# Another order of the seven outer products in the down projection of a retention + SwiGLU kernel, with split inner sums and a last unit that is finished block by block

## The chip, the cores and the metric

The kernel runs on one core of a Trainium2 chip. A core has five engines that each work through their own list of instructions in order: TensorE (PE in the profile; its weight loads are PEld), VectorE (DVE), ScalarE (ACT), GpSimd (POOL) and SyncE (SP, which here only issues transfers). They wait for one another through semaphores. Matmuls write to PSUM, eight banks of 128 x 512 f32; everything else lies in SBUF. The metric is the device time of one execution in microseconds (us).

## The reference, cut to what matters

```python
# q, k, v: (8 batches, 8 heads, 576 positions, 64), f32
scores = q @ k.T / sqrt(64);  ret = scores * gamma_h ** (i - j)  for j <= i, else 0
x = (ret @ v) as (8*576 = 4608 tokens, 8*64 = 512 channels)
xn = x / sqrt(mean(x*x) + 1e-6) * rms_g
h = silu(xn @ w_gate) * (xn @ w_val)      # 4608 x 1536
out = h @ w_out                           # 4608 x 512
```

Nearly all of the arithmetic is in the two projections of the last two lines.

## The kernel before, in words

**Units.** The 4608 tokens are worked through in nine units of 512 (u = 0 to 8). A unit has an up part (gate and value projection, six groups `up(u, n)`) and a down part, `across(u)`. Attention for later units is done in slots between the up groups. All program text from `start` on is under a manual schedule: the order in which the Python emits instructions is the order on each engine. Units 0 and 1 take their up part plainly (`up_plain`, L664), while the weights are still being rounded and combined; this front is emitted by the string `PLAN`, whose entries stand for pieces of work: `w` and `a` steps of weight rounding on VectorE and ScalarE, `U` a plain up group (u, k, n), `S` an attention slot, `d` differences of h, `i` inner sums of unit 0, `W36` "all 36 weight halves joined", `A0`/`A1` the next half outer product of unit 0 or 1, `R2 Y2 X2 M2` the normalisation of unit 2 and its mixtures. For units 2 to 8 a loop (from L1113) takes over.

**Seven products in place of eight.** A 2x2 block product is formed with seven block products (Winograd's form of Strassen's scheme). Down is done so on two levels. Outer: h (128 x 12 x 512) is read as b11, b12, b21, b22 (channel halves by token halves), and the operands of the seven outer products are A11 = b11, A12 = b21, S4 = b22, S1 = b12 − b11 (in the spare tile t1, `differences`, L688), S3 = b22 − b12 (in b12's place, same line), S2 = S3 + b11 (overwrites b11 after the first product, L803), and A22 = b21 − S2 (overwrites t1 after the second, L805). In `operands_of` this is a table from name to tile. Inner: every outer operand is itself split in four, of which three quarters are used raw and four are sums i1, i3, i2, i4, made by `inner_sums(u, n)`, four operations over 128 x 384 (three channel blocks of 128 tokens). Sums lie in `inner[:, 0 or 1]` in turn, those of the third product in `sums_x`. From unit 2 on they run on GpSimd, those of n = 1 on VectorE (`eng`, L720).

**An outer product** is 21 matmuls of 128 x 128 x 128 over three channel blocks (L749): first the three raw quarters (18 records in the trace), then the four sums (24 records), accumulating into seven 128 x 128 places in a pair of PSUM banks, `o` with four places and `p` with three. So `zo<-ring,t` is the product whose raw operand is t1, and `zo<-ring,vi` its part on inner sums. Banks are called x, z, w, y, and the order of n = 0 to 6 on them is x z w y x z w: a repeated letter accumulates onto the earlier product. ScalarE copies x to the f32 tile `vec` (`keep`, L763); VectorE adds the other banks (`add`, L770). Four blocks of `vec` then hold the inner products of the four output blocks, which `combine` turns into out rows: seven 128 x 512 additions on GpSimd, for the last unit seven 128 x 128 additions per block on VectorE (L848). `store` writes them, on SP's queue, in the last unit also on ScalarE's.

**What sets the order.** Weight blocks stream through a ring in SBUF: `pieces` lists them in order of use, `refill` (L573) issues a transfer on SP when the place is free. When an inner sum, a bank or a tile of h is overwritten, the writer waits for the last reader. `across(u)` yields between half products, so that front and loop can put other work between: of the next unit root and normalisation (L521), mixtures (`sums_of_x`, L533).

```python
nm = "xzwyxzw"[n]
product(n, nm, w, False)                     # raw quarters
product(n, nm, w, True)                      # inner sums
if u > 1 and n in (0, 1, 3, 4):
    inner_sums(u, {0: 3, 1: 4, 3: 5, 4: 6}[n])   # sums of a later product
```

Of the kernel before, what the change touches and what calls it, by code (L numbers as in the profile page):

```python
# [41 lines left out]
def kernel(  # L42
# [499 lines left out]
    ORDER = (A11, S1, S3, S2, A12, S4, A22)  # L542
    pieces = [("out", 0, n) for n in range(7)] + [("out", 1, n) for n in range(3)]
# [13 lines left out]
    def refill(most=len(pieces)):  # L557

        nonlocal n_sent
        while n_sent < min(most, len(pieces)):  # L560
# [7 lines left out]
            if kind == "up":  # L568
                src = w_up_d[n]
            else:  # L570
                o = o.rearrange("p (c x) -> p c x", c=NK)
                src = w_out_d[ORDER[n]].rearrange("c p x -> p c x")
# [3 lines left out]
    def piece(kind, u, n):  # L576
        i = pieces.index((kind, 0 if kind == "out" and u == 1 and n > 2 else u, n))
# [111 lines left out]

    def s2_of(u):  # L690
        return flat_t[1].rearrange("p (f t) -> p f t", t=HU)

    def operands_of(u):
# [4 lines left out]
        other = s2_of(1), flat_t[0].rearrange("p (f t) -> p f t", t=HU)  # L698
        s2, a22 = other if u == 1 else (b11, t1)
        return {A11: b11, S1: t1, S3: b12, S2: s2, A12: b21, S4: b22, A22: a22}  # L700

    def inner_of(u, n):
        if u > 1 and n == 2:
            t = sums_x.rearrange("p i c t -> p (i c t)")
            return list(t.rearrange("p (i c t) -> i p c t", i=4, c=NK))
        at = (0, 1, None, 0, 1, 0, 1)[n] if u > 1 else (7 * u + (n + 4 * u) % 7) % 2
        return [inner[:, at, i] for i in range(4)]

    def inner_sums(u, n):

        x = operands_of(u)[ORDER[n]]
# [3 lines left out]
        eng = nc.vector if (n == 1 if u > 1 else 7 * u + (n + 4 * u) % 7 in (4, 7, 10, 12)) else nc.gpsimd  # L715
        for o, a, b, op in (
            (i1, x12, x11, ALU.subtract), (i3, x22, x12, ALU.subtract),
            (i2, i3, x11, ALU.add), (i4, x21, i2, ALU.subtract),
        ):
            eng.tensor_tensor(out=o, in0=a, in1=b, op=op)  # L720

    def across(u):
# [8 lines left out]
        first = set()  # L731

# [4 lines left out]
        def product(n, nm, w, late):  # L737
# [3 lines left out]
            x = operands[ORDER[n]]  # L741
# [19 lines left out]
        def keep(b, nm):  # L761
            for o, ps in parts(vec[:, b], nm):
                nc.scalar.copy(out=o, in_=ps)  # L763
# [7 lines left out]

        last = u == NU - 1
        if u > 1:
            for n in range(3):
                inner_sums(u, n)
        yield
        for i, n in enumerate((3, 4, 5, 6, 0, 1, 2) if u == 1 else range(7)):
            nm = "xzwyxzw"[n]
            w = piece("out", u, n)
            product(n, nm, w, False)  # L780
# [4 lines left out]
            if u == 1:  # L785
                if i in (2, 3):
                    for at, v in ((0, "x"), (3, "y")) if i == 2 else ((2, "z"), (1, "w")):
                        keep(at, v)
                        first.difference_update([(v, 0), (v, 1)])
                elif n == 0:  # L790
                    add(0, 0, "x")
                    add(3, 3, "x")
                    plus(1, 3)
                    plus(2, 3)
                elif n == 1:
                    add(2, 2, "z")
                    add(3, 3, "z")
                elif n == 2:
                    add(1, 1, "w")
                    add(3, 3, "w")  # L800
            elif n == 0:
                keep(3, "x")
                nc.vector.tensor_tensor(out=b11, in0=b12, in1=b11, op=ALU.add)  # L803
            elif n == 1:
                nc.vector.tensor_tensor(out=t1, in0=b21, in1=b11, op=ALU.subtract)  # L805
            elif n == 3:
                add(1, 3, "y")
                add(3, 1, "z")
                add(3, 3, "w")
                if last:  # L810
                    combine(3)
            elif n == 4:
                keep(0, "x")
                if last:
                    combine(0)
            elif n == 5:
                add(2, 1, "z")
                if last:
                    combine(2)
            elif n == 6:  # L820
                add(1, 1, "w")
                if last:
                    combine(1)
            if u == 0 and n == 3:
                o = operands_of(1)
                nc.vector.tensor_tensor(out=o[S2], in0=o[A11], in1=o[S3], op=ALU.add)
            elif u == 0 and n == 6:
                nc.vector.tensor_tensor(out=o[A22], in0=o[A12], in1=o[S2], op=ALU.subtract)
            if u > 1:
                if n in (0, 1, 3, 4):  # L830
                    inner_sums(u, {0: 3, 1: 4, 3: 5, 4: 6}[n])
            elif 7 * u + i + 2 < 14:
                v, i = divmod(7 * u + i + 2, 7)
                inner_sums(v, (i + 3) % 7 if v else i)
# [16 lines left out]

    def store(u, b=None):
# [3 lines left out]
        for i, (n, r, c) in enumerate(((A12, 0, 0), (S4, 0, 1), (S3, 1, 1), (A22, 1, 0))):  # L856
# [3 lines left out]
            else:  # L860
                queue = nc.scalar if i % 2 else nc.sync
                queue.dma_start(out=rows[c][r][:, b // 2, b % 2], in_=vec[:, b, n])
# [112 lines left out]
    def finish_slice(k):  # L975
# [3 lines left out]
            (w_out_d[o][k], slices[:, o].rearrange("p n d -> p (n d)")) for o in ORDER  # L979
        ]))  # L980

    def store_blocks(n):
# [17 lines left out]
        a1 U132 a1 w1 U133 a1 w1 w1 w1 w1 w1 U040 U041 F10 w1 a1 w1 w1 U042 a1 a1 a1 a1 a1 a1 a1  # L1000
        a1 w1 w1 w1 U043 a1 a1 a1 a1 w1 w1 U050 a1 a1 a1 w1 a1 a1 a1 w1 U051 w1 a1 a1 a1 w1 a1
        w1 U052 a1 w1 U053 w1 a1 w1 w1 w1 W36 U140 a1 a1 a1 S8 P10 U141 S9 F11 a1 a1 U142 z0
        U143 a1 a1 a1 r1 a1 a1 a1 a1 a1 d1 d0 a1 U150 a1 a1 a1 a1 S10 U151 a1 r2 P11 U152 a1 a1
        i0 d2 U153 a1 A0 d5 d4 a1 S11 i1 A0 d3 A0 C11 r99 A0 A0 A0 a1 Q8 A0 G8 Q9 A0 Q10 F12 G9
# [158 lines left out]
```

## Time and profile before

| what | value |
|---|---|
| time, median of 3 runs | 1126.14 us (1125.84 to 1126.41) |
| profiled execution | 1123.96 us, span 1122.0, granted TensorE clock 0.996 |
| start of across in unit 0, 1, 4, 8 | 237.5, 273.9, 513.9, 1082.7 |
| an outer product that waits for nothing | 4.69 us |
| last matmul ends, last VectorE operation ends | 1115.5, 1119.3 |
| last store issued, landed | 1119.3, 1120.9 |

Times in the rows are microseconds from the start of the span. A timeline row gives start, length, engine, line and operation, `out<-in`, the shape, the number of instructions drawn together, and in brackets the idle time before it and what ended that. A row of stretches gives, from a start to an end, the length and then for each engine its busy time with the number of instructions, the TensorE clock (1.00 is full), DMA share and GB/s. `tile` rows give the number, the least, median and greatest duration in ns, and the first and last start. Units 2 to 7 are the middle units; unit 4 stands for them in the rows shown.

### The profile page before, as it was taken

What the parts mean: (1) busy time and instruction counts of PE and PEld (TensorE: products, weight loads), DVE (VectorE), ACT (ScalarE), POOL (GpSimd) and SP (SyncE); (2) the same over time, 40 slices, a digit from 0 to 9 for tenths busy, and PEclk for the clock granted to TensorE, in tenths of its full rate; (3) what the DMA queues carried; (4) which work ended last, traced back from release to release, by engine and by line L of the source; (5) the groups of instructions that cost most, each with busy time, mean ns of one, the idle gap of its engine ahead of it and who ended that gap; (6) DMA issues with size and microseconds to landing.
All of it is one profiled execution on the core that took longest, in us unless ns stands there. A gap on an engine that the chain in (4) does not pass through costs nothing. (4 is left out here: it accounts for less than half of the span.)

```text
span 1122.0 us, 24228 instructions
## 1 busy us (share of the span) xinstructions
PE 1095.8 (98%) x10102; PEld 914.7 (82%) x10102; DVE 797.6 (71%) x1383; ACT 272.9 (24%) x551; POOL 397.5 (35%) x328
## 2 busy tenths in 40 slices
PE   8799999999999999999999999999999999999997
PEld 7654444579988899889988898889888998898897
DVE  4768767997777795769577777778576935594465
ACT  5656465211112301121122202130122011201110
POOL 0024526566630065005800391028301740183035
PEclk8999999999999999999999999999999999999999
DMA  8765888697778965796678865997475755575361
GB/s 187 205 176 196 321 199 274 204 333 188 266 270 235 231 235 213 176 233 237 232 218 191 284 250 136 241 262 279 131 202 192 269 195 175 187 271 170 139 246 38
DMA packets 253868, 243.70 MB, mean 217 GB/s; under 512 B 193088, under 2 KB 213824, under 8 KB 247616
## 3 DMA queue, kind: packets, MB, share of 16 engines
q1 hardware_dynamic: 252176, 241.61, 69.6%
q8 instruction: 79, 1.29, 0.5%
q10 hardware_dynamic: 1584, 0.56, 0.2%
q14 instruction: 29, 0.24, 0.1%
HBM read 212.05 MB, written 30.08 MB: 216 GB/s over the span
## 5 line engine op out<-in xcount | busy, mean ns | idle before, releaser
L720 POOL TENSOR_TENSOR vi<-h 128x384 f32<-128x384 f32 x64 | 76.7, 1214 | 484.3 <-DVE h L623 451.4
L664 PE MATMUL up<-x,ring 128*128 128x512 f32 x384 | 166.6, 594 | 0.8 <-DVE x L521 0.8
L604 PE MATMUL x<-x,ring 128*128 128x256 f32 x672 | 161.4, 383 | 0.0
L604 PE MATMUL w<-sums,ring 128*128 128x256 f32 x672 | 159.3, 380 | 0.0
L604 PE MATMUL z<-x,ring 128*128 128x256 f32 x672 | 158.8, 379 | 0.0
L664 PEld LDWEIGHTS up<-x,ring 128*128 128x128 f32 x384 | 72.4, 190 | 90.5 <-issue 84.2
L604 PEld LDWEIGHTS z<-x,ring 128*128 128x128 f32 x672 | 127.7, 190 | 19.9 <-issue 2.9
L604 PEld LDWEIGHTS w<-sums,ring 128*128 128x128 f32 x672 | 127.3, 190 | 17.4
L604 PEld LDWEIGHTS x<-x,ring 128*128 128x128 f32 x672 | 125.1, 190 | 17.3
L604 PE MATMUL y<-sums,ring 128*128 128x256 f32 x336 | 79.4, 379 | 0.0
L848 POOL TENSOR_TENSOR vi<-vi 128x512 f32<-128x512 f32 (+1 forms) x56 | 67.4, 1215 | 25.2 <-DVE vi L770 22.7
L611 DVE TENSOR_TENSOR h<-u,w 128x512 f32<-128x512 f32 x42 | 28.9, 688 | 66.0 <-PE w L604 49.1
L604 PEld LDWEIGHTS y<-sums,ring 128*128 128x128 f32 x336 | 63.9, 190 | 8.7
L630 ACT COPY m<-x 128x512 f32<-128x512 f32 x42 | 24.6, 585 | 187.1 <-PE x L604 187.1
L611 DVE TENSOR_TENSOR u<-m,y 128x512 f32<-128x512 f32 x42 | 28.7, 684 | 48.1 <-PE y L604 48.1
L763 ACT COPY vi<-xo 128x512 f32<-128x512 f32 x17 | 10.0, 585 | 215.9 <-PE xo L749 178.9
L625 ACT ACTIVATE h<-h 128x512 f32<-128x512 f32 x63 | 39.5, 629 | 85.1 <-DVE h L611 85.1
L334 DVE SCALAR_TENSOR_TENSOR sum<-sum,gc,s 128x64 f32<-128x64 f32 x192 | 53.9, 281 | 6.8
L961 POOL TENSOR_TENSOR vi<-vi 128x512 f32<-128x512 f32 (+1 forms) x24 | 40.7, 1697 | 37.8 <-DVE vi L950 23.8
L611 DVE TENSOR_TENSOR u<-u,z 128x512 f32<-128x512 f32 x42 | 28.9, 688 | 25.5 <-PE z L604 24.4
L720 POOL TENSOR_TENSOR vi<-h,vi 128x384 f32<-128x384 f32 x32 | 44.7, 1396 | 2.5
L961 POOL TENSOR_TENSOR ring<-ring 128x512 f32<-128x512 f32 x24 | 30.5, 1273 | 42.2 <-DVE ring L950 31.8
(256 smaller groups left out, 1992.8 us busy)
## 6 DMA issues: line engine op xcount, KB each, us to landing
ring<-w_out_blocks SPq DMA_DIRECT2D x59, 1344.0 KB, 6.4
ring<-w_up_blocks SPq DMA_DIRECT2D x42, 1792.0 KB, 7.7
w_out_blocks<-vi SPq DMA_DIRECT2D x21, 448.0 KB, 5.7
out_dram<-vi SPq DMA_DIRECT2D x64, 128.0 KB, 2.9
qraw<-in_q_dram SPq DMA_DIRECT2D x96, 72.0 KB, 4.3
kraw<-in_k_dram SPq DMA_DIRECT2D x96, 72.0 KB, 3.2
k<-in_k_dram SPq DMA_DIRECT2D x48, 128.0 KB, 2.9
v<-in_v_dram SPq DMA_DIRECT2D x48, 128.0 KB, 3.0
```

The costliest lines, as they stand in the source:

```text
L334: nc.vector.scalar_tensor_tensor(out=t[:, c], in0=t[:, c - 1], scalar=gc[:, hp : hp + 1], in1=part, op0=ALU.mult, op1=ALU.add,)
L604: nc.tensor.matmul(ps[:, i * HU : i * HU + HU], lhsT=w[:, PLACE[blk], c, i * P : i * P + P], rhs=t_of[u][blk][:, c], start=(start and i == ...
L611: nc.vector.tensor_tensor(out=o, in0=a, in1=pairs_of(ps), op=ALU.add)
L625: nc.scalar.activation(out=o, in_=c, func=AF.Silu)
L630: nc.scalar.copy(out=s1, in_=pairs_of(x_))
L664: nc.tensor.matmul(ps, lhsT=w[:, PLACE[blk], c % 2, i * P : i * P + P], rhs=x_of[u][:, c], start=(c == 0), stop=(c == NHP - 1),)
L720: eng.tensor_tensor(out=o, in0=a, in1=b, op=op)
L763: nc.scalar.copy(out=o, in_=ps)
L848: eng.tensor_tensor(out=t[:, :, o], in0=t[:, :, x], in1=t[:, :, y], op=ALU.add)
L961: nc.gpsimd.tensor_tensor(out=t[o], in0=t[x], in1=t[y], op=op)
```

## The change

The outer products come in another order: A11, S4, A12, S1, S2, S3, A22 for units 0 to 7 (unit 1 begins with its fourth, S1), and A11, A12, S2, S3, S1, S4, A22 for unit 8. Banks are assigned anew: x z x z y w x in the middle units, where the third product (n = 2) continues on the first's bank and a copy (`keep`) with sign −1 takes z; `plus` adds one block of `vec` to another (128 x 896). The first two products' inner sums are made in two parts, channel block 0 (with all of i1) already in the last up group but one of the unit (n = 4), channel blocks 1 and 2 when across starts; all inner sums from unit 2 on are on GpSimd but one set of unit 8. In unit 8 output block 0 is finished after the second product straight from PSUM, block 3 after the fifth, block 2 after the sixth on GpSimd, block 1 piece by piece while the last product still runs: its seven inner products take PSUM places of their own. `PLAN` is written anew in its second half. The diff, cut:

```diff
+    LAST_ORDER = (A11, A12, S2, S3, S1, S4, A22)
+
+    def order_of(u):
+        if u == 1:
+            return FIRST_ORDER[3:] + FIRST_ORDER[:3]
+        return LAST_ORDER if u == NU - 1 else FIRST_ORDER
+
+    pieces = [("out", 0, n) for n in range(7)] + [("out", 1, n) for n in range(4, 7)]
     N_FIRST = len(pieces)
     for u in range(2, NU):
         pieces += [("up", u, n) for n in range(2 * NG)] + [("out", u, n) for n in range(7)]
...
-        i = pieces.index((kind, 0 if kind == "out" and u == 1 and n > 2 else u, n))
+        if kind == "out" and u == 1 and n < 4:
+            i = pieces.index(("out", 0, n + 3))
+        else:
+            i = pieces.index((kind, u, n))
...
+        s2, a22 = b11, t1
+        if u == 1:
+            s2, a22 = s2_of(1), flat_t[0].rearrange("p (f t) -> p f t", t=HU)
+        elif u == NU - 1:
+            if not of_last:
+                of_last.extend(xp.tile([P, NHP, U], F32, tag="x", name=nm) for nm in ("s2", "a22"))
+            s2, a22 = (
+                t.rearrange("p c t -> p (c t)")[:, : NH * HU].rearrange("p (f t) -> p f t", t=HU)
+                for t in of_last
+            )
...
-        if u > 1 and n == 2:
+        if u > 1 and n == 2 or u == NU - 1 and n == 6:
             t = sums_x.rearrange("p i c t -> p (i c t)")
             return list(t.rearrange("p (i c t) -> i p c t", i=4, c=NK))
-        at = (0, 1, None, 0, 1, 0, 1)[n] if u > 1 else (7 * u + (n + 4 * u) % 7) % 2
+        at = (0, 1, None, 0, 1, 0, 1)[n] if u > 1 else (7 * u + n) % 2
...
+    def inner_sums(u, n, part=None):
+
+        x = operands_of(u)[order_of(u)[n]]
         x11, x12 = x[:, :NK, :P], x[:, :NK, P:]
         x21, x22 = x[:, NK:, :P], x[:, NK:, P:]
         i1, i3, i2, i4 = inner_of(u, n)
-        eng = nc.vector if (n == 1 if u > 1 else 7 * u + (n + 4 * u) % 7 in (4, 7, 10, 12)) else nc.gpsimd
+        on_vector = u < 2 and 7 * u + n in (4, 7, 10, 12) or (u, n) == (NU - 1, 2)
+        eng = nc.vector if on_vector else nc.gpsimd
+        if part != 1:
+            eng.tensor_tensor(out=i1, in0=x12, in1=x11, op=ALU.subtract)
+        c = slice(1, NK) if part == 1 else slice(0, 1) if part == 0 else slice(0, NK)
         for o, a, b, op in (
-            (i1, x12, x11, ALU.subtract), (i3, x22, x12, ALU.subtract),
-            (i2, i3, x11, ALU.add), (i4, x21, i2, ALU.subtract),
+            (i3, x22, x12, ALU.subtract), (i2, i3, x11, ALU.add), (i4, x21, i2, ALU.subtract),
         ):
-            eng.tensor_tensor(out=o, in0=a, in1=b, op=op)
+            eng.tensor_tensor(out=o[:, c], in0=a[:, c], in1=b[:, c], op=op)
...
+        ANEW = {(1, 4), (1, 5), (NU - 1, 5)} | {(i, 6) for i in range(NU - 1) if i != 1}
...
-        def keep(b, nm):
+        def keep(b, nm, sign=1.0):
             for o, ps in parts(vec[:, b], nm):
-                nc.scalar.copy(out=o, in_=ps)
+                if sign == 1.0:
+                    nc.scalar.copy(out=o, in_=ps)
+                else:
+                    nc.scalar.activation(out=o, in_=ps, func=AF.Copy, scale=sign)
+
+        def anew(nm):
+            first.difference_update([(nm, 0), (nm, 1)])
...
+        def before_last(b):
+
+            sums = early["t"] = temp("before_last").rearrange("p (n d) -> p n d", n=4)
+            part = temp("parts_last").rearrange("p (n d) -> p n d", n=4)
+            for o, x, y in (
+                (sums[:, 0], block(b, A11), block(b, A12)), (part[:, 0], block(b, A11), block(b, S2)),
+                (part[:, 1], part[:, 0], block(b, S1)), (sums[:, 1], part[:, 1], block(b, S4)),
+                (sums[:, 2], part[:, 1], block(b, S3)), (part[:, 2], part[:, 0], block(b, S3)),
+                (sums[:, 3], part[:, 2], block(b, A22)),
+            ):
+                plus_to(o, x, y)
+
+        def combine_of_bank(b, nm):
+
+            ps = [vector[nm][s // 4][:, s % 4 * P : s % 4 * P + P] for s in range(7)]
+            nc.scalar.copy(out=block(b, A11), in_=ps[A11])
+            for o, x, y in (
+                (S2, A11, S2), (S1, S2, S1), (A12, A11, A12), (A11, S2, S3), (S3, S1, S3),
+                (S4, S1, S4), (A22, A11, A22),
+            ):
+                plus_to(block(b, o), block(b, x), ps[y])
+            store(NU - 1, b)
+
+        def last_product(w):
...
+            order = (A11, S2, S1, S3, A12, S4, A22)
+            room = {s: vector["yywwzz"[i]][i % 2][:, :P] for i, s in enumerate(order[:6])}
+            room[A22] = vector["y"][0][:, P : 2 * P]
+            for s in order:
+                ps = room[s]
+                for i in range(NK):
+                    nc.tensor.matmul(
+                        ps, lhsT=lhs[s][:, i], rhs=w[:, s, i], start=(i == 0), stop=(i == NK - 1),
+                        skip_group_check=True,
+                    )
+                if s == A11:
+                    nc.scalar.copy(out=c1, in_=ps)
+                    plus_to(a12, a12, c1)
+                elif s == S2:
+                    plus_to(c2, c1, ps)
...
+                elif s == A12:
+                    plus_to(o[A12], a12, ps)
+                    store_part(1, A12, nc.scalar)
...
+                else:
+                    plus_to(o[A22], a22, ps)
+                    store_part(1, A22, nc.scalar)
...
         if u > 1:
-            for n in range(3):
-                inner_sums(u, n)
+            for n, part in ((0, 1), (1, 1)) if last else ((0, 1), (1, 1), (2, 0), (2, 1)):
+                inner_sums(u, n, part)
+        if last:
+            nc.vector.tensor_tensor(out=operands[S2], in0=b12, in1=b11, op=ALU.add)
+            inner_sums(u, 2)
+            nc.vector.tensor_tensor(out=operands[A22], in0=b21, in1=operands[S2], op=ALU.subtract)
         yield
-        for i, n in enumerate((3, 4, 5, 6, 0, 1, 2) if u == 1 else range(7)):
-            nm = "xzwyxzw"[n]
+        banks_in_turn = "zywxzwz" if u == 1 else "xxywzx." if last else "xzxzywx"
+        for n, nm in enumerate(banks_in_turn):
             w = piece("out", u, n)
+            if last and n == 6:
+                last_product(w)
+                yield
+                continue
+            if nm in banks_in_turn[:n] and (u, n) in ANEW:
+                anew(nm)
             product(n, nm, w, False)
             yield
             product(n, nm, w, True)
             if u != 0 or n < 3:
                 used()
             if u == 1:
...
+                if n == 2:
+                    keep(2, "z")
+                    keep(0, "y")
+                elif n == 3:
+                    keep(1, "w")
+                    add(3, 2, "w")
+                    add(1, 1, "x")
+                elif n == 4:
+                    add(0, 0, "z")
+                    for i in (2, 1, 3):
+                        plus(i, 0)
+                elif n == 5:
+                    add(2, 2, "w")
+                elif n == 6:
+                    keep(0, "z")
+            elif last:
+                if n == 0:
+                    keep(1, "x")
                 elif n == 1:
-                    add(2, 2, "z")
+                    combine_of_bank(0, "x")
+                elif n == 2:
+                    add(1, 1, "y")
+                elif n == 3:
+                    add(3, 1, "w")
+                    before_last(3)
+                elif n == 4:
                     add(3, 3, "z")
-                elif n == 2:
-                    add(1, 1, "w")
-                    add(3, 3, "w")
+                    add(2, 1, "z")
+                    combine(3)
+                elif n == 5:
+                    add(2, 2, "x")
+                    combine(2, nc.gpsimd)
             elif n == 0:
-                keep(3, "x")
+                keep(1, "x")
                 nc.vector.tensor_tensor(out=b11, in0=b12, in1=b11, op=ALU.add)
             elif n == 1:
+                keep(3, "z", -1.0)
+            elif n == 2:
+                keep(0, "x")
+            elif n == 3:
                 nc.vector.tensor_tensor(out=t1, in0=b21, in1=b11, op=ALU.subtract)
-            elif n == 3:
-                add(1, 3, "y")
-                add(3, 1, "z")
+            elif n == 4:
+                add(1, 1, "y")
+                add(2, 1, "z")
+                plus(3, 2)
+            elif n == 5:
                 add(3, 3, "w")
-                if last:
-                    combine(3)
-            elif n == 4:
...
+                add(1, 1, "w")
             elif n == 6:
-                add(1, 1, "w")
-                if last:
-                    combine(1)
-            if u == 0 and n == 3:
-                o = operands_of(1)
+                add(1, 1, "x")
+            o = operands_of(1)
+            if (u, n) == (0, 3):
                 nc.vector.tensor_tensor(out=o[S2], in0=o[A11], in1=o[S3], op=ALU.add)
-            elif u == 0 and n == 6:
+            elif (u, n) == (0, 6):
                 nc.vector.tensor_tensor(out=o[A22], in0=o[A12], in1=o[S2], op=ALU.subtract)
             if u > 1:
-                if n in (0, 1, 3, 4):
-                    inner_sums(u, {0: 3, 1: 4, 3: 5, 4: 6}[n])
-            elif 7 * u + i + 2 < 14:
-                v, i = divmod(7 * u + i + 2, 7)
-                inner_sums(v, (i + 3) % 7 if v else i)
+                ahead = {0: 3, 1: 4, 2: 6, 3: 5} if last else {0: 3, 1: 4, 3: 5, 4: 6}
+                if n in ahead:
+                    inner_sums(u, ahead[n])
+            elif 7 * u + n + 2 < 14:
+                inner_sums(*divmod(7 * u + n + 2, 7))
             yield
...
         combine_blocks([slices[:, i, :4] for i in range(7)], S1)
         combine_blocks([slices[:, :, i] for i in range(7)], S1)
         stores.append((n_joined + 5, [
-            (w_out_d[o][k], slices[:, o].rearrange("p n d -> p (n d)")) for o in ORDER
+            (w_out_d[o][k], slices[:, o].rearrange("p n d -> p (n d)")) for o in FIRST_ORDER
         ]))
...
-        a1 U132 a1 w1 U133 a1 w1 w1 w1 w1 w1 U040 U041 F10 w1 a1 w1 w1 U042 a1 a1 a1 a1 a1 a1 a1
-        a1 w1 w1 w1 U043 a1 a1 a1 a1 w1 w1 U050 a1 a1 a1 w1 a1 a1 a1 w1 U051 w1 a1 a1 a1 w1 a1
-        w1 U052 a1 w1 U053 w1 a1 w1 w1 w1 W36 U140 a1 a1 a1 S8 P10 U141 S9 F11 a1 a1 U142 z0
-        U143 a1 a1 a1 r1 a1 a1 a1 a1 a1 d1 d0 a1 U150 a1 a1 a1 a1 S10 U151 a1 r2 P11 U152 a1 a1
-        i0 d2 U153 a1 A0 d5 d4 a1 S11 i1 A0 d3 A0 C11 r99 A0 A0 A0 a1 Q8 A0 G8 Q9 A0 Q10 F12 G9
-        a1 G10 A0 a1 A0 A0 A0 P12 a1 Q11 A0 A0 A0 A0 F13 A1 G11 A1 k0 o0 A1 A1 A1 A1 A1 R2 A1 A1
-        A1 Y2 A1 X2 A1 M2 A1 A1 A1 A1
+        a1 U132 a1 w1 U133 a1 w1 w1 w1 w1 w1 w1 U040 a1 U041 F10 w1 a1 w1 a1 a1 a1 a1 a1 a1 w1
+        a1 U042 a1 w1 w1 a1 a1 a1 w1 U043 a1 w1 a1 a1 U050 a1 w1 w1 a1 a1 U051 U052 w1 w1 w1 w1
+        U053 a1 w1 w1 w1 a1 w1 a1 U140 W36 S8 a1 a1 a1 P10 U141 a1 S9 a1 a1 U142 F11 A0 a1 U143
+        a1 a1 a1 a1 z0 a1 d0 r1 a1 a1 a1 i0 d1 a1 S10 a1 a1 a1 P11 a1 a1 a1 U150 U151 a1 U152
+        S11 Q8 r2 U153 a1 i1 a1 d5 a1 d2 r99 A0 A0 A0 d3 C11 A0 A0 d4 G8 Q9 G9 A0 a1 A0 Q10 A0
+        k0 F12 G10 A0 A0 A0 a1 P12 A0 a1 A0 A0 F13 A0 Q11 G11 A1 A1 A1 o0 A1 A1 A1 A1 A1 A1 R2
+        A1 A1 A1 Y2 X2 M2 A1 a1 A1 A1 A1
...
                 for i, _ in enumerate(up(u, n)):
                     if n == 1 and i == 4:
                         store(u - 1)
+                    if n == 2 * NG - 2 and i == 1:
+                        inner_sums(u, 0, 0)
+                        inner_sums(u, 1, 0)
```

## The prediction

> **What bounds the kernel now.** First the page's busy times, to see which engine is full:
>
> ```profile
> PE 1095.8 (98%) x10102; PEld 914.7 (82%) x10102; DVE 797.6 (71%) x1383; ACT 272.9 (24%) x551; POOL 397.5 (35%) x328
> ```
>
> TensorE is the bound and its matmuls are neither removed nor added, so the change can win only idle time on it. Next the stretches of the span (first number after the length: TensorE's busy us), to see where that idle time lies:
>
> ```profile
> 0.00:100.00 100.00, 88.18 (x1430) 59.57 (x1431) 65.64 (x172) 57.36 (x128) 13.68 (x25) 0.97 0.72 196
> 200.00:300.00 100.00, 97.48 (x1131) 78.33 (x1130) 83.51 (x146) 16.72 (x39) 64.11 (x52) 1.00 0.75 238
> 500.00:600.00 100.00, 99.33 (x950) 90.09 (x949) 74.57 (x123) 18.92 (x39) 38.99 (x31) 1.00 0.73 221
> 1100.00:1122.00 22.00, 15.68 (x141) 15.49 (x139) 15.84 (x38) 0.97 (x2) 9.41 (x10) 0.97 0.17 48
> ```
>
> The first stretch isn't touched; 200 to 300, the middle and the tail are. Then TensorE's waits by what ended them (total, times, longest):
>
> ```profile
> PE zp L749 <- DVE vi L720: 2.0, 6, 0.3
> PE zo L749 <- DVE vi L720: 2.0, 6, 0.3
> PE xp L749 <- issue: 1.0, 1, 1.0
> ```
>
> Six times each, once per middle unit: the second outer product waits for its inner sums on VectorE. These totals are too small, as the starts in unit 4 show (timeline):
>
> ```profile
> 518.59 1.50 PE L749 MATMUL zo<-ring,t 128*128 128x128 f32 x12
> 521.33 1.24 DVE L720 TENSOR_TENSOR vi<-vi,t 128x384 f32<-128x384 f32 x1
> 522.60 1.24 DVE L720 TENSOR_TENSOR vi<-t,vi 128x384 f32<-128x384 f32 x1
> 522.62 0.94 PE L749 MATMUL zp<-ring,vi 128*128 128x128 f32 x6 [0.34 <-DVE vi L720]
> 523.89 0.94 PE L749 MATMUL zo<-ring,vi 128*128 128x128 f32 x6 [0.34 <-DVE vi L720]
> 524.66 1.50 PE L749 MATMUL wo<-ring,h 128*128 128x128 f32 x12
> ```
>
> The product takes 524.66 − 518.59 = 6.07 us; its neighbours 4.69 (513.90 to 518.59 before it, 524.66 to 529.35 behind it). Stall: 1.38 us.
>
> **Step 1, middle units (2 to 7).** The second and third outer products become S4 and A12, whose operands are b22 and b21, parts of h that are ready as they are, and the channel-0 part of the sums of the first two products goes to GpSimd inside the last up group but one. The 1.38 us goes six times: **−8.3** (−7.5 to −8.5). GpSimd gets a third more sums. From the rows:
>
> ```profile
> L720 POOL TENSOR_TENSOR vi<-h x64: 992/1010/2576, 229.2 to 1102.4; 128x384 f32<-128x384 f32 x64
> L720 DVE TENSOR_TENSOR vi<-t x16: 546/950/1356, 285.4 to 1086.0; 128x384 f32<-128x384 f32 x16
> ```
>
> one sum is 1.01 us on GpSimd against 0.55 on VectorE (minimum). The Trainium skill ("GPSIMD Engine Reference", section 4.1) speaks against this move: two-input elementwise work about 2x slower there. The row says 1.8x. If GpSimd's queue were the path, 24 sums moved would cost 24 x 0.46 = +11 us; but it is busy 35%. Counting from the across start: the third product's sums are done at 7.1 us; then four sets, which in unit 4 took 6.55, 5.3, 4.75 and 5.0, so 28.7, and the last product reads its sums at 6 x 4.69 + 2.0 (raw matmuls) + 2.0 (first inner sums later) ≈ 32.1. Margin 3.4; each set also lands before its own product. I cost it at nothing. VectorE loses four sums (some 4.3 us) per unit and gains one 128x896 add (1.1), ScalarE two copies more (1.07 us, 24% busy): hidden. S2's update of b11 stays behind the first product, A22's moves behind the fourth, two products before its use. The weight pieces are fetched in the new order with the same lead (they landed 12 us or more ahead), so SP's queue costs nothing.
>
> The pace of the sets depends on sharing. The skill ("SBUF — State Buffer", section Who interferes with whom) has VectorE with two SBUF inputs exclude GpSimd's reads. The rows fit: a 128x384 sum goes from 1.00 to 1.33 and up to 2.4 us on GpSimd, while adds with a PSUM input stay at 0.68. Were every sum as slow as full exclusion by 1.37-us VectorE operations (2.4 us), a set would take 9.6 and the last product wait some 13 us; the measured sets stand at 5.4. I take the sets, since VectorE's mix hardly changes.
>
> **Step 2, front (weight rounding and the last up groups of unit 1).** The written order now puts the SwiGLU multiplications of three groups ahead of the last weight halves on VectorE.
>
> ```profile
> 207.56 0.75 DVE L950 SCALAR_TENSOR_TENSOR vi<-ring,exp 128x256 f32<-128x256 f32 x2
> ```
>
> This last join ends at 208.3; three multiplications (0.69 each) before it put it at 210.3. The attention step S8 follows a later bank release (+1.0), U141 the joins (+0.5), S9 a little: **+1.6** (0 to +2.5). GpSimd's combines of weights start 2 us later; their stores end at 229.7 instead of 227.7, before unit 0's products read the pieces.
>
> **Step 3, unit 0.** The 1.0 "issue" wait in its first product (1.15 by starts) came with an instruction packet at 239.1. U153 now lies between S11 and that product, so the code is fetched elsewhere, behind matmuls that don't wait: **−1.15** (0 to −1.2).
>
> **Step 4, unit 1 into unit 2.** Here the change adds a wait. TensorE starts unit 2's up products at 309.73, 35.84 behind unit 1's first product (273.89), and wants the third operation of M2 1.7 later (37.56);
>
> ```profile
> 309.24 0.69 DVE L533 TENSOR_TENSOR sums<-x 128x512 f32<-128x512 f32 x1
> 309.73 1.89 PE L604 MATMUL x<-x,ring 128*128 128x256 f32 x8
> ```
>
> shows it just in time. After: on VectorE behind the fourth product (end 20.9 from unit 1's start) stand two adds (2.4), four sums (2.2), three normalisation operations (2.1), one add (1.2), three 128x896 adds (3.4, behind the fifth product), two operations of Y2 (1.4), X2 (2.7) and three of M2 (2.2): 38.6. Stall 1.0 undisturbed; with four sums contended at 1.24 instead of 0.56, 3.7. Queued behind are M2's last operation and the next unit's mixtures, which follow at once. Between: **+2.3** (+0.5 to +4). The third product's 2.15 us stall in unit 1 stays, as GpSimd's combine still precedes its sums.
>
> **Step 5, last unit.** The second product accumulates into the bank that ScalarE is just copying: 0.25 + 0.585 + 0.07 = +0.9 on TensorE. Before, the end was VectorE's:
>
> ```profile
> 1114.85 0.83 PE L749 MATMUL wo<-ring,vi 128*128 128x128 f32 x6
> 1117.29 1.99 DVE L848 TENSOR_TENSOR vi<-vi 128x128 f32<-128x128 f32 x7
> ```
>
> matmuls end at 1115.5, then two adds and seven combines to 1119.3, 36.6 behind the last across start (1082.7). After: matmuls end at 33.0 + 0.9 − 0.16 = 33.7 (0.16 was an old stall in the last product), then one VectorE piece (0.3 to 0.7): 34.5. Block 2 on GpSimd has seven 128x128 operations, which no row shows: below, VectorE's 0.29; above, contended 0.8; a 128x512 takes 1.27 and 384 take 1.00, so 0.27 per 128 columns over a fixed 0.19 gives 0.46 (an estimate). From 29.0 + 1.4 (adds) they take 3.7: 34.1, contended 35. Stores of 64 KB follow as before. I take 34.8: **−1.8** (−0.5 to −2.5).
>
> **Sum.** −8.3 + 1.6 − 1.15 + 2.3 − 1.8 = −7.35 against the profiled span of 1122.0 (execution 1123.96, clock 0.996). The median of runs lies 2.2 above that execution; what is removed is a difference, so 1126.14 − 7.35 = **1118.8**.
>
> **Rivals.** *The front keeps up*: steps 2 and 4 cost nothing, because the order was only rearranged around the same VectorE work: −8.3 − 1.15 − 1.8 = −11.3, 1114.9. For it: VectorE is less loaded; against: 83.5% busy from 200 to 300, the fullest stretch. *The front stalls more*: both at their upper ends, the fetch wait kept, tail at −0.5: −8.3 + 2.5 + 4 − 0.5 = −2.3, 1123.8; with part of it, about 1123. *GpSimd becomes the bound*, the other side: sets longer than (32.1 − 7.1)/4 = 6.25 us make the last product wait four times the excess in six units. At 6.55 (the slowest set seen, at 525.65) that is 4 x 0.3 x 6 = 7.2 and the whole gain is gone; from 6.65 it is slower, at 7.0 +18 − 7.35: 1137. Against it: the mean is 5.4. *The stall only moves*: the removed wait reappears at the third product, because S1's place was the only thing early; then steps 2 to 5 alone, +1: 1127. Against it: A12 and S4 are complete when across begins.
>
> **How the numbers follow.** Measurement tells 0.2%, 2.25 us, from no change. Likeliest case (1116.8 to 1121): 0.51. Front keeps up (1113.5 to 1116.8): 0.22. Front stalls more (1121 to 1123.9): 0.18. Stall only moves (1124 to 1128): 0.04. GpSimd bound (above 1128.4): 0.05. From 1114.5 to 1123.0 lie some 0.8. Faster 0.91, same 0.04, slower 0.05.
>
> **What would show it.** Right: in the middle units no product over 4.8 us and no wait of z on line 720; GpSimd's sets about 5.4 and idle before the last product; waits near 206 to 212 and at unit 2's first up group of about 2 us each; the last operation 34.8 behind the last across start. Wrong: a product at the end of across waiting for GpSimd, larger waits near 206 to 230, a chain through GpSimd at the end.

## The result, and the profile after

The changed kernel takes **1116.24 us** (median of 4 runs, 1115.18 to 1118.5) against 1126.28 beside it (1125.84 to 1127.21): ratio 0.9912, 95% interval 0.9895 to 0.993, so 10.0 us less; the forecast of 1118.8 was 2.6 us too high. Its profiled execution took 1118.5, span 1116.6, clock 0.994; this span is only 5.4 us below the one before, because its start-up took longer (first row of the stages below).

Busy times of the page after:

```profile
PE 1093.8 (98%) x10102; PEld 915.3 (82%) x10102; DVE 798.5 (72%) x1367; ACT 279.9 (25%) x565; POOL 467.8 (42%) x419
```

GpSimd has 70 us more work; VectorE lost and gained about the same. TensorE's waits after, cut to the ones that matter:

```profile
PE y L614 <- DVE sums L533: 0.9, 1, 0.9
PE wp L773 <- POOL vi L743: 0.8, 2, 0.5
PE xo L773 <- ACT vi L788: 0.7, 1, 0.7
PE last L305 <- DVE sums L1069: 0.6, 1, 0.6
PE up L674 <- DVE vi L1086: 0.5, 1, 0.5
```

The rows of z on VectorE (six times each) are gone. Single ones are left or new: unit 2's mixtures (y), unit 1's sums behind the combine (wp), the last unit's copied bank (xo), the front (last, up). Unit 4 in the timeline, its second product and the two GpSimd operations that end the third product's and the last set's sums:

```profile
522.01 1.50 PE L773 MATMUL zo<-ring,h 128*128 128x128 f32 x12
523.84 2.12 POOL L743 TENSOR_TENSOR sums<-h,sums 128x256 f32<-128x256 f32 x1
526.70 1.50 PE L773 MATMUL xo<-ring,h 128*128 128x128 f32 x12
547.48 1.00 POOL L743 TENSOR_TENSOR vi<-t,vi 128x384 f32<-128x384 f32 x1
```

526.70 − 522.01 = 4.69: no stall. Stage by stage, by the starts of the first matmuls in the two profiles (after minus before; "again" is a second profile of the same kernel):

| stage | predicted | after | again |
|---|---|---|---|
| span's start to the 41st of 48 plain up groups (U140) | 0 | +3.05 | +3.88 |
| from there to unit 0's across (step 2) | +1.6 | +1.96 | +1.96 |
| unit 0 (step 3) | −1.15 | −1.56 | −1.56 |
| unit 1, and unit 2's up groups (step 4) | +2.3 | +0.22, +1.33 | +0.22, +1.40 |
| across of units 2 to 7 (step 1) | −8.3 | 6 x −1.38 = −8.3 | −8.3 |
| up groups of units 3 to 8 | 0 | −0.2 | +0.4 |
| last across to the end of the span (step 5) | −1.8 | +0.98 on TensorE, −2.84 behind it | +0.98, −2.81 |

Behind the start-up the changed kernel is 8.4 us ahead, 7.35 were forecast. The start-up's difference is there at the third of these groups already (68.8 and 71.9), ahead of everything that the change touches; in the fourteen profiles taken, that group began anywhere from 68.8 to 73.3. That is more than most of the steps weigh, so what follows is judged by stages, and by medians only where they differ by several microseconds.

### The profile page after: what moved, and what is told of

Same layout as the page of the kernel before. It is cut to its first block, busy times and chain, and to the rows that moved or that the text cites. A ratio compares the mean times of both kernels' runs of the same rounds, so it can differ in the third digit from the quotient of the medians.

```text
span 1116.6 us, 24381 instructions
## 1 busy us (share of the span) xinstructions
PE 1093.8 (98%) x10102; PEld 915.3 (82%) x10102; DVE 798.5 (72%) x1367; ACT 279.9 (25%) x565; POOL 467.8 (42%) x419
## 3 DMA queue, kind: packets, MB, share of 16 engines
q8 instruction: 79, 1.29, 0.5%
## 4 chain that ended last, share of the span: by engine, by line
PE 90%; DVE 6%; issue 1%; POOL 1%; ACT 1%; DMA 0%; SPq 0%; POOLq 0%; DVEq 0%; ACTq 0%
PE up L674 14%; PE x L614 13%; PE z L614 13%; PE w L614 13%; PE y L614 7%; PE xo L773 6%; PE xp L773 4%; PE zo L773 3%; PE zp L773 3%; PE yo L773 2%; PE av L355 2%; PE wo L773 2%; PE s L285 2%; PE av L375 2%; PE yp L773 1%
## 5 line engine op out<-in xcount | busy, mean ns | idle before, releaser
L738 POOL TENSOR_TENSOR vi<-h 128x384 f32<-128x384 f32 x32 | 38.9, 1217 | 288.6 <-DVE h L633 273.3
L743 POOL TENSOR_TENSOR vi<-h 128x384 f32<-128x384 f32 (+2 forms) x46 | 48.0, 1042 | 147.0 <-DVE h L633 147.0
L977 POOL TENSOR_TENSOR vi<-vi 128x512 f32<-128x512 f32 (+2 forms) x63 | 71.9, 1153 | 35.4 <-DVE vi L800 32.6
L1097 POOL TENSOR_TENSOR vi<-vi 128x512 f32<-128x512 f32 (+1 forms) x24 | 40.7, 1698 | 40.7 <-DVE vi L1086 26.8
L743 POOL TENSOR_TENSOR vi<-vi,h 128x384 f32<-128x384 f32 (+2 forms) x46 | 48.9, 1062 | 3.6
L743 POOL TENSOR_TENSOR vi<-h,vi 128x384 f32<-128x384 f32 (+2 forms) x46 | 46.2, 1005 | 3.6
```

The costliest lines, as they stand in the source:

```text
L738: eng.tensor_tensor(out=i1, in0=x12, in1=x11, op=ALU.subtract)
L743: eng.tensor_tensor(out=o[:, c], in0=a[:, c], in1=b[:, c], op=op)
L977: eng.tensor_tensor(out=t[:, :, o], in0=t[:, :, x], in1=t[:, :, y], op=ALU.add)
L1097: nc.gpsimd.tensor_tensor(out=t[o], in0=t[x], in1=t[y], op=op)
```

## The experiments

**1. Which part of the change takes the 1.38 us away?** Four runs take apart the order, the split of the sums and the engine of the second product's sums. Where the split goes, it goes in unit 8 too, whose end comes 0.6 us later for it. First, the changed kernel with these sums on VectorE.

```diff
-on_vector = u < 2 and 7 * u + n in (4, 7, 10, 12) or (u, n) == (NU - 1, 2)
+on_vector = u < 2 and 7 * u + n in (4, 7, 10, 12) or (u, n) == (NU - 1, 2) or (1 < u < NU - 1 and n == 1)
```

> The changed kernel, with the inner sums of the second product (S4) of units 2 to 7 back on VectorE, their two parts as they are. Theory (the order gives the gain: S4 and A12 are ready early): all four sums are there before TensorE reads them, since b22 is complete some 3 us ahead of across; no stall comes back, the second product stays at 4.69 us, the time at about 1116 (within 2 us of the changed kernel). Rival (the move to GpSimd gives it): the product waits again for VectorE, 1.4 us six times, about 1124.5.

Measured: 1117.82 (1116.37 to 1120.31), ratio 0.9925 (0.9908 to 0.9943); no product of a middle unit over 4.69. The move to GpSimd is not what gives the gain. Second, the changed kernel without the split:

```diff
-for n, part in ((0, 1), (1, 1)) if last else ((0, 1), (1, 1), (2, 0), (2, 1)):
+for n, part in ((0, None), (1, None)) if last else ((0, None), (1, None), (2, None)):
...
 if n == 2 * NG - 2 and i == 1:
-    inner_sums(u, 0, 0)
-    inner_sums(u, 1, 0)
+    pass
```

> The changed kernel, with the inner sums of the first three products made whole when across starts and nothing of them in the up group before. Theory (the order gives the gain): in the trace of the changed kernel GpSimd is idle until 512.25, 5 us ahead of across, so whole sums are done at about 516.9 and 521.5, needed from 519.3 and 524.0 on: nothing is lost, 1116 to 1118. Rival (the split is what takes the sums off the path): the first or second product waits 0.5 to 1.4 us in each middle unit, 1120 to 1125.

Measured: 1123.57 (1121.99 to 1127.6), ratio 0.998 (0.997 to 0.9991). My theory's number was wrong: 1.07 us come back in each middle unit. The second product is still free (4.69), so they are not where the rival had them either, but at the fifth (0.23), sixth (0.61) and seventh product (0.22). Timeline of unit 4 in this run: the end of the third product's sums, the sixth product's last set on TensorE (x12 at 1.70 in place of 1.50), and the last sum.

```profile
523.41 2.40 POOL L743 TENSOR_TENSOR sums<-h,sums 128x384 f32<-128x384 f32 x1
541.62 1.70 PE L773 MATMUL wp<-ring,vi 128*128 128x128 f32 x12
547.33 1.00 POOL L743 TENSOR_TENSOR vi<-t,vi 128x384 f32<-128x384 f32 x1
```

Across starts at 515.25 here: the third product's sums end 10.5 behind it, 1.9 later than in the changed kernel (525.96 − 517.33 = 8.6), the last sum 33.1 instead of 31.1. GpSimd's queue ends 2.0 us later and that costs 1.07, so about 1.0 was spare. Third, the kernel before with the engine alone changed:

```diff
-        eng = nc.vector if (n == 1 if u > 1 else 7 * u + (n + 4 * u) % 7 in (4, 7, 10, 12)) else nc.gpsimd
+        eng = nc.vector if (u == NU - 1 and n == 1 if u > 1 else 7 * u + (n + 4 * u) % 7 in (4, 7, 10, 12)) else nc.gpsimd
```

> The kernel before, with only the engine changed: the second product's inner sums (S1) of units 2 to 7 on GpSimd. Theory: with the old order the operand t1 is ready only 5.6 us after the start of across; four operations of 1.2 us on GpSimd end later than VectorE's, and the third product's sums queue behind them: the second product's stall grows from 1.38 to 1.9 or more and later products may wait 0.4 to 0.7; slower than before by 3 to 13 us (1129 to 1139). Rival (the engine gives the gain): 1118.

Measured: 1143.26 (1141.59 to 1143.66), ratio 1.0146 (1.0131 to 1.0162), 17 us slower: beyond my range, since I had put little on the queue behind. The second product stalls 1.83, the third 1.99 and the fourth 0.26, because the later sums wait behind the second's (timeline, unit 4):

```profile
525.15 1.44 POOL L720 TENSOR_TENSOR vi<-t 128x384 f32<-128x384 f32 x1 [5.33 <-DVE t L688]
530.41 2.85 POOL L720 TENSOR_TENSOR sums<-h 128x384 f32<-128x384 f32 x2
```

GpSimd stands idle for 5.33 us before t1 is ready, and then is late for the rest. Last, the order alone: the edits of the first two runs together.

```diff
-on_vector = u < 2 and 7 * u + n in (4, 7, 10, 12) or (u, n) == (NU - 1, 2)
+on_vector = u < 2 and 7 * u + n in (4, 7, 10, 12) or (u, n) == (NU - 1, 2) or (1 < u < NU - 1 and n == 1)
...
-for n, part in ((0, 1), (1, 1)) if last else ((0, 1), (1, 1), (2, 0), (2, 1)):
+for n, part in ((0, None), (1, None)) if last else ((0, None), (1, None), (2, None)):
...
-    inner_sums(u, 0, 0)
-    inner_sums(u, 1, 0)
+    pass
```

> The changed kernel, with the second product's sums on VectorE and nothing split or made early: of the change in units 2 to 7 only the order of the products is left. Theory (the order is what takes the stall away, the split only pays for the larger load of GpSimd): GpSimd has a set of some 5 us less, so the last products don't wait; VectorE comes to the sums some 6 us behind the start of across, needed from 6.7 on: at most 0.5 us lost in each unit, 1116 to 1119. Rival (without an early part the second product waits whatever the order): 1 us or more in each unit, 1122 or more.

Measured: 1135.0 (1134.56 to 1136.42), ratio 1.0078 (1.0064 to 1.0092): slower than before. Each second product loses 2.87 us, more than the 1.38 of the old order. My theory fell again. Timeline of unit 4, TensorE and VectorE:

```profile
523.06 1.50 PE L773 MATMUL zo<-ring,h 128*128 128x128 f32 x12
524.63 1.35 DVE L738 TENSOR_TENSOR vi<-h 128x384 f32<-128x384 f32 x1
526.03 0.94 PE L773 MATMUL zo<-ring,vi 128*128 128x128 f32 x6 [0.80 <-DVE vi L738]
530.62 1.50 PE L773 MATMUL xo<-ring,h 128*128 128x128 f32 x12
```

The operand b22 is complete 2.1 us before across starts (516.30 and 518.37), but on VectorE the sums stand behind the last multiplications and both differences, and begin 6.3 us after that start. With the parts (first run, across starts at 519.14) the same engine reaches them hardly sooner, 5.2 us behind the start, yet has only three of 128x256 left:

```profile
524.38 0.94 DVE L743 TENSOR_TENSOR vi<-h 128x256 f32<-128x256 f32 x1
525.84 0.83 PE L773 MATMUL zo<-ring,vi 128*128 128x128 f32 x6
526.22 1.10 DVE L743 TENSOR_TENSOR vi<-h,vi 128x256 f32<-128x256 f32 x1
```

The whole of i1 and the first channel block of the others are there, so TensorE begins at 525.84 and never catches up with the rest. Stall per middle unit, all products together:

| order | second product's sums on | made | stall, us |
|---|---|---|---|
| old | VectorE | whole | 1.38 |
| old | GpSimd | whole | 4.08 |
| new | VectorE | whole | 2.87 |
| new | GpSimd | whole | 1.07 |
| new | VectorE | in two parts | 0 |
| new | GpSimd | in two parts | 0 |

Neither the order nor the engine does it: alone each makes the stall longer, together they leave 1.07. With the early part it is gone on either engine. Whether the old order would do with early parts as well was not run. t1's first channel blocks are formed two up groups earlier than its last, so early parts are possible there. An estimate from the two traces: in the old order VectorE reaches the sums 0.89 us behind the product's start (519.48 − 518.59); three operations of 128x256 took it 2.94 in the first run (524.38 to 527.32), so they would end 3.83 behind that start, and there the last of them was not read before 4.02 (527.85 − 523.83). By this the new order would not be needed for the 1.38. It stays open.

The kernel before has one more case on record, unit 8: same order, same engine, whole sums, and no stall (1087.38 to 1092.07 is 4.69). VectorE has no root and normalisation of a next unit there, and begins the sums 2.9 us behind the start of across (1082.69), in unit 4 5.6 us behind it (513.90):

```profile
519.48 1.82 DVE L720 TENSOR_TENSOR vi<-t 128x384 f32<-128x384 f32 x2
1085.55 1.82 DVE L720 TENSOR_TENSOR vi<-t 128x384 f32<-128x384 f32 x2
```

So the old stall, too, goes with what stands ahead of the sums in VectorE's queue. To put them ahead of the next unit's root was not tried.

**2. How near is GpSimd to being the bound?** The changed kernel with one sum of the sixth and one of the seventh product formed twice.

```diff
-eng.tensor_tensor(out=i1, in0=x12, in1=x11, op=ALU.subtract)
+for _ in range(2 if 1 < u < NU - 1 and n in (5, 6) else 1):
+    eng.tensor_tensor(out=i1, in0=x12, in1=x11, op=ALU.subtract)
```

> The changed kernel, with the first sum of the sixth and seventh product's set formed twice on GpSimd in units 2 to 7: two operations of 1.0 to 1.44 us more in a queue whose last set ends 31.1 us behind the start of across. By the prediction's sum GpSimd has 3.4 us to spare: no stall, 1116. By the run with whole sums (there the last sums ended 33.1 us behind the start of across, and 1.07 us were lost) only 1.0 is left: the last product, or the last two, wait about 2.4 - 1.0 = 1.4 us in each of six units, +8.4, 1124.5.

Measured: 1125.26 (1123.34 to 1127.26), ratio 0.9988 (0.9979 to 0.9997); 1.30 us are lost in the last product of each middle unit. Two operations of 1.0 to 1.44 make 2.4, so 1.1 was spare, as the run with whole sums had it. The prediction's 3.4 is refuted.

**3. The front.** The changed kernel with the whole of the old string `PLAN` (its second half differs; two cuts):

```diff
...
-        U053 a1 w1 w1 w1 a1 w1 a1 U140 W36 S8 a1 a1 a1 P10 U141 a1 S9 a1 a1 U142 F11 A0 a1 U143
+        w1 U052 a1 w1 U053 w1 a1 w1 w1 w1 W36 U140 a1 a1 a1 S8 P10 U141 S9 F11 a1 a1 U142 z0
...
-        A1 A1 A1 Y2 X2 M2 A1 a1 A1 A1 A1
+        A1 Y2 A1 X2 A1 M2 A1 A1 A1 A1
```

> The changed kernel with the written order of the front (the string PLAN) as before. By the steps of the prediction: the multiplications no longer stand ahead of the last joins, -1.9 us between the up groups and unit 0; the fetch wait in unit 0's first product comes back, +1.2; unit 1 into unit 2 between -1.1 and +1. Net -2 to +0.5 against the changed kernel, 1114 to 1117. Rival (the new front is needed by the new order, or pays): a wait of 2 us or more in units 0 and 1 that the changed kernel doesn't have, 1119 or more.

Measured: 1118.94 (1117.43 to 1119.58). By stages against the kernel before: +0.65 to unit 0's across (changed kernel +1.96), +0.80 in unit 0 (−1.56), +0.32 and +2.19 on the way through unit 1 and unit 2's up groups (+0.22, +1.33). The first gained 1.3 of the 1.9 expected; unit 0 lost 2.36 where 1.2 was expected, the rest 0.96, the bad end of its range. By these stages the old order loses 2.0 in all. Of unit 0's 2.36, 1.05 are in the first product and 1.3 in the attention step beside the second (its last 32 matmuls took 2.00 instead of 0.69). Two of its waits:

```profile
PE y L614 <- DVE sums L533: 1.7, 1, 1.7
PE xp L773 <- issue: 0.7, 1, 0.7
```

The issue wait is back at the place it had before (0.87 by starts, 1.15 before). So step 3 is shown as far as this: the wait follows what is issued ahead of the product. That U153 alone does it was not run. Then the old order only up to S9:

```diff
...
-        a1 U042 a1 w1 w1 a1 a1 a1 w1 U043 a1 w1 a1 a1 U050 a1 w1 w1 a1 a1 U051 U052 w1 w1 w1 w1
-        U053 a1 w1 w1 w1 a1 w1 a1 U140 W36 S8 a1 a1 a1 P10 U141 a1 S9 a1 a1 U142 F11 A0 a1 U143
+        w1 w1 w1 U043 a1 a1 a1 a1 w1 w1 U050 a1 a1 a1 w1 a1 a1 a1 w1 U051 w1 a1 a1 a1 w1 a1 w1
+        U052 a1 w1 U053 w1 a1 w1 w1 w1 W36 U140 a1 a1 a1 S8 P10 U141 S9 U142 F11 A0 a1 U143 a1 a1
...
```

> The changed kernel, with the written order of the front as before up to and with S9, as in the change behind it. Theory (what the old front is better in is the part up to S9 alone; what the new one is better in lies behind): A0 starts 1.3 us earlier relative to the up groups as in the run with the whole old order, and unit 0 and the way into unit 2 stay as in the changed kernel: -1.3 us, 1115. Rival (the late multiplications come back at another place): a new wait of about 1.3 us before unit 0's first product, no gain.

Measured: 1115.68 (1114.59 to 1117.62), beside 1117.24 for the changed kernel on that chip. To unit 0's across +1.29: 0.67 of the expected 1.3 came back, all of it at S8 (0.91 lost there became 0.24); the 0.53 before U141 and the 0.42 in S9 stayed, and unit 0 kept its gain. The traces show what holds these two. VectorE has its old queue again, but one of its joins now waits for a store, which the same join in the kernel before (second row) does not:

```profile
200.89 0.42 DVE L1086 SCALAR_TENSOR_TENSOR vi<-ring,exp 128x256 f32<-128x256 f32 x1 [2.08 <-DMA w_out_blocks<-vi]
197.37 0.75 DVE L950 SCALAR_TENSOR_TENSOR vi<-ring,exp 128x256 f32<-128x256 f32 x2
```

The join overwrites the combined weight block of S1, which must have been stored first. The change stores the seven blocks in the new product order (`FIRST_ORDER` in `finish_slice`), so S1's goes out fourth instead of second; the join starts as the fourth store lands (200.87). Counted from U140's start, VectorE's last join ends at 6.98 before, 8.83 in the changed kernel, 8.16 here and 7.62 with the whole old order, where the same wait is 1.54. TensorE's loss on the way to unit 0 follows: 0, 1.96, 1.29, 0.65. In the changed kernel VectorE does not pause for more than 0.1 us from 201.15 to the last join's end at 213.2, so there the three multiplications ahead of the joins cost the 1.85 us; with them moved away, the wait for the store takes part of their place. The new order with the old order of stores was not run.

**4. Unit 1 into unit 2.** Unit 1's three additions of 128x896 behind the mixtures:

```diff
 elif n == 4:
     add(0, 0, "z")
-    for i in (2, 1, 3):
-        plus(i, 0)
...
 elif n == 6:
+    for i in (2, 1, 3):
+        plus(i, 0)
     keep(0, "z")
```

> The changed kernel, with unit 1's three additions of 128x896 moved from behind its fifth product to behind its seventh, so that the mixtures of unit 2 stand ahead of them on VectorE. Theory: the wait of unit 2's second up product for VectorE (1.07 us in the trace) goes, -1.1 us between unit 1 and unit 2, 1115. Rival (a wait takes its place: the copy of z, now behind the additions, gives its bank late): a new wait of 1 us or more in unit 2's first up groups, no gain.

Measured: 1116.73 (1116.3 to 1117.86). The wait moved and kept most of its size: 0.99 instead of 1.33 are lost between unit 2's first up group and its across. A line of the waits and two of the timeline:

```profile
PE x L614 <- ACT m L640: 0.8, 1, 0.8
312.28 3.10 DVE L796 TENSOR_TENSOR vi<-vi 128x896 f32<-128x896 f32 x3
315.46 0.58 ACT L788 COPY vi<-zo 128x512 f32<-128x512 f32 x1 [13.58 <-DVE vi L796]
```

ScalarE's copy of z waits for the additions, and the copy of unit 2's first bank stands behind it. Then the third product's sums of unit 1 on VectorE, out from behind GpSimd's combine:

```diff
-7 * u + n in (4, 7, 10, 12)
+7 * u + n in (4, 7, 9, 10, 12)
```

> The changed kernel, with the inner sums of unit 1's third product on VectorE, where they don't stand behind GpSimd's combine of 7.4 us. Theory: the stall of 2.38 us in that product goes, -2.4 us, 1114; VectorE's other work of unit 1 is at most 2.2 to 5 us later, and has an idle gap of 2.9 us ahead of the sixth product. Rival (VectorE becomes late): the wait comes back in unit 1's later products or grows from 1.07 us before unit 2's second up product, gain under 1 us.

Measured: 1115.88 (1114.13 to 1116.43). The stall went from 2.38 to 1.12, now for VectorE; half of what was expected, and nothing given back.

**5. The end.** Block 2 of the last unit on VectorE:

```diff
-combine(2, nc.gpsimd)
+combine(2)
```

> The changed kernel, with block 2 of the last unit combined on VectorE. Theory (the end is VectorE's queue): seven operations of 0.29 us stand ahead of the last pieces, of which some 0.4 fall into an idle gap: the last operation 1.6 us later (36 instead of 34.3 behind the last across start), 1117.8. Rival (the stores' landing or TensorE sets the end): within 0.3 us of the changed kernel by the trace.

Measured: 1118.33 (1117.34 to 1119.47). The span ends 39.1 behind the last across start (1078.26) instead of 37.5: the 1.6 expected, though by another way. VectorE's last operation is 1.2 later, and its last results now come 0.2 us apart, while their four stores leave ScalarE's queue one every 0.48 us, so that the last one is issued 0.9 us behind the last operation instead of 0.2:

```profile
1113.20 1.82 ACTq L997 DMA_DIRECT2D out_dram<-vi  x4
1113.48 0.28 DVE L806 TENSOR_TENSOR vi<-before_last,yo 128x128 f32<-128x128 f32 x1
```

**6. A faster version?** The front as before up to S9, unit 1's third sums on VectorE, and the three additions on GpSimd ahead of the sixth product's add:

```diff
-on_vector = u < 2 and 7 * u + n in (4, 7, 10, 12) or (u, n) == (NU - 1, 2)
+on_vector = u < 2 and 7 * u + n in (4, 7, 9, 10, 12) or (u, n) == (NU - 1, 2)
...
 elif n == 4:
     add(0, 0, "z")
-    for i in (2, 1, 3):
-        plus(i, 0)
 elif n == 5:
+    for i in (2, 1, 3):
+        plus(i, 0, nc.gpsimd)
     add(2, 2, "w")
```

> The changed kernel, with the front as before up to S9 (-1.3), the inner sums of unit 1's third product on VectorE (-1.25 as measured alone), and unit 1's three additions of 128x896 on GpSimd behind its sums (the wait of 1.07 us for the mixtures goes; GpSimd is free from its last sums of unit 1 on). Theory: the three add up, -3.6 us between the up groups of unit 1 and those of unit 2, 1112.6. Rival (one of them turns into a new wait): gain under 2 us.

Measured: 1117.59 (1116.69 to 1120.98), no better than the changed kernel beside it. The way through unit 2's up groups costs 3.34 instead of 1.33. Its longest wait, and VectorE's root and normalisation of unit 2 (L502, then L521; 0.69 and 2.74 us in the changed kernel) while GpSimd adds:

```profile
PE y L614 <- DVE sums L533: 2.0, 1, 2.0
303.01 7.51 POOL L796 TENSOR_TENSOR vi<-vi 128x896 f32<-128x896 f32 x3
303.64 2.45 DVE L502 SCALAR_TENSOR_TENSOR sq<-e,sq 128x512 f32<-128x512 f32 x1
306.12 6.26 DVE L521 SCALAR_TENSOR_TENSOR x<-x,rms_k,sq 128x512 f32<-128x512 f32 x4
```

The front and the sums on VectorE without the third edit would by their stages give 0.67 + 1.25 = 1.9 us (an estimate); that version was not run. The changed kernel itself once more, on that chip, is the measure for this series:

> The changed kernel once more, on the same chip as the others, as their measure: 1116 within 1.5 us, with stage times within 0.1 us of its first profile behind the start-up (up groups to unit 0 +1.96 against the kernel before, unit 0 -1.56, unit 1 +0.22, middle units -1.38 each, last unit +0.98 on TensorE).

Measured: 1117.24 (1116.88 to 1120.0), stages as in the table.

## Why the prediction was right, and where not

- **Step 1.** The size was right to the hundredth (six times 1.38). Its reasoning was not: "parts of h that are ready as they are" is not enough (order alone: 2.87 lost). Order and GpSimd together free the second product, but hand 1.07 to the fifth to seventh; what takes these away is the early part, which the prediction named in half a sentence. Nor was A12's operand b21 complete "when across begins": VectorE finished it at 521.44, 4.1 us behind the start, and only b22 was. GpSimd's sums grew from 24 to 28 in a unit, a sixth and not "a third more". "I cost it at nothing" for GpSimd held by 1.0 us, not 3.4: the third product's sums ended at 8.6, not 7.1 (GpSimd idle for 0.63 until VectorE had the last of b21, then operations of up to 2.12), and the four sets took 5.6, 6.7, 5.3 and 5.0, mean 5.64 instead of 5.4. So the sign "idle before the last product" did not come true, and the rival "GpSimd becomes the bound" was nearer than its 0.05: with 8.6 its limit is (32.1 − 8.6)/4 = 5.9 for a set, not 6.25.
- **Step 2.** +1.96 for +1.6, by the way forecast: VectorE's last join came 1.85 us later (2.0 forecast), S8 lost 0.91 (1.0), U141 0.53 (0.5), S9 0.42 ("a little"). "Front keeps up" was wrong. The prediction did not count the new order of the stores; in the changed kernel it costs nothing, because the multiplications hide it.
- **Step 3.** −1.34 in the first product, −1.56 for the unit with the attention step beside it; −1.15 forecast, at most −1.2. The whole old front brought 0.87 of the wait back.
- **Step 4.** The mixture is ready 316.06 − 277.34 = 38.7 behind unit 1's first product; the undisturbed sum was 38.6. The mis-sized term is the contention added to it: stall 1.07, I took 2.3. The four sums it feared for, those of unit 1's sixth product, took 0.55 to 0.56 each and were not slowed by their neighbours here.
- **Step 5.** TensorE +0.98 for +0.9; the last operation 34.3 behind the last across start (34.8), GpSimd's seven 128x128 operations 3.54 us (3.7 forecast).

```profile
1109.94 3.54 POOL L977 TENSOR_TENSOR vi<-vi 128x128 f32<-128x128 f32 x7 [5.78 <-DVE vi L800]
1113.19 0.29 DVE L806 TENSOR_TENSOR vi<-before_last,yo 128x128 f32<-128x128 f32 x1 [0.38 <-PE yo L850]
```

Both engines end at 1113.5. Of the 1.05 us by which the sum fell short behind the start-up, step 4 makes 0.75 and unit 0 0.4, against 0.36 in the front; the rest is 0.2 of the up groups. The medians differ by 10.0, and by 9.1 in the second measurement; what of that goes beyond the stages' 8.4 no profile locates.

## What to carry to other kernels

An operand that is ready early helps only if the instruction that reads it stands early in its engine's queue: a new order of work pays when the queue is rearranged with it, here by making a first part of the sums in the last up group but one. When a stall is removed by loading an engine that "has time", count that engine's queue against the last reader of the stage and not its busy share: 42% busy left 1 us in 31. Test each part of a combined change alone, since here two of the parts made it slower by themselves.

## What was not expected of the hardware

GpSimd's 128x896 additions more than doubled VectorE's normalisation beside them (6.26 us against 2.74 for the same four operations), so that work taken off VectorE slowed it. Each of the three additions (2.53 us) held up one VectorE operation, which took 2.45 to 2.56 us instead of 0.69 to 0.75: the one of L502 and the first two of L521; the last two of L521, behind the additions, took 0.74. The operations have two SBUF inputs (e and sq, x and sq), and the Trainium skill ("SBUF — State Buffer", Who interferes with whom) has just these share a read port with GpSimd; the measured size, 5.3 us over 7.5 us of GpSimd's work, ate what the edit was to bring. And the start-up, with unchanged instructions up to the third plain group, varied by 4.5 us from profile to profile; the granted clock of the first 100 us (0.93 to 1.00) doesn't order these (69.7 at 0.95, 71.2 at 0.98). What makes it vary is open.
